# A linear-attention and gated-FFN block rewritten around a static list schedule: K and V first with in-place features, Q feature-major, attention output token-major

## The chip, the cores and the metric

Both kernels run on one core of one Trainium2 chip. The metric is the device time of one execution in microseconds (us). All outputs are right.

Five engines work side by side and meet through semaphores: TensorE (PE in the profile; PEld is its weight loads), VectorE (DVE), ScalarE (ACT), GpSimd (POOL), and SyncE (SP), which only issues DMAs. SPq and ACTq are the instruction streams in which SP and ACT issue them. Each engine works through the list that the program gives it, and in these traces an instruction that waits holds up what is listed behind it on that engine.

## The reference

With B=1, S=2048, D=640, H=32 heads of width 20, F=1536, all in bf16:

```python
def A(x, wqkv, w_phi, wo):                       # linear attention
    q, k, v = split_heads(x @ wqkv)              # each [H, S, 20]
    pq, pk = q @ w_phi, k @ w_phi                # per head, 20x20
    phi_q = concat(softmax(pq), softmax(-pq))    # softmax over the head's 20 features
    phi_k = concat(softmax(pk), softmax(-pk))
    kv  = phi_k^T @ v                            # [40, 20] per head, a sum over ALL tokens
    z   = phi_k.sum(tokens)
    o   = (phi_q @ kv) / (phi_q @ z + 1e-6)
    return merge_heads(o) @ wo

def B(x, w_gate, w_up, w_down):                  # bilinear gated FFN
    return ((x @ w_gate) * (x @ w_up)) @ w_down

h   = x + A(layernorm(x))
out = h + B(layernorm(h))
```

The sum over all tokens in `kv` is a barrier: no attention output exists before the last tile of K and V is done. Tokens are handled in 16 tiles of 128. Both kernels fold `w_phi` into the Q and K weights at the start ("the fold"), so that one projection gives `pq` and `pk` directly.

## The kernel before

The kernel is written by hand, engine by engine. Per tile, TensorE projects Q, K and V in one group of 1,920 columns. VectorE takes a row maximum of |pq| and |pk|, which ScalarE uses as the bias of four exponentials. VectorE then forms the feature sums of K and of Q, 1.39 to 1.41 us each, and their reciprocals. GpSimd normalises. The Q features are token-major at this point, so SyncE transposes them by two DMAs a tile.

```python
# SyncE: one semaphore "trq" counts both transposes of a tile
def trq(t):
    be = t % 3
    W(sy, "ex", 4 * t + 1)
    W(sy, "trq", 32 * t)                 # until BOTH transposes of tile t-1 have landed
    I(sy.dma_start_transpose(phiqT[:, 0, :, P*t:P*(t+1)], e_tmp[:, be, 0, :]), "trq", 16)
    W(sy, "nq", t + 1)
    W(sy, "trq", 32 * t + 16)            # until the first transpose of tile t has landed
    I(sy.dma_start_transpose(phiqT[:, 1, :, P*t:P*(t+1)], e_tmp[:, be, 1, :]), "trq", 16)

# VectorE
def emit_ss(t):
    ...
    dve.tensor_reduce(out=Ssum[:, b, 0:2*H], in_=phik[:, t, ...], op=ALU.add)          # K sums
    k = I(dve.tensor_reduce(out=Ssum[:, b, 2*H:4*H], in_=e_tmp[:, t%3, ...], op=ALU.add), "ss")  # Q sums
    ...                                                                               # reciprocals
for t in range(NT):
    W(dve, "prj", t + 1)
    I(dve.tensor_reduce(out=mx[:, t, :], in_=pp[:, 0:2*D]..., op=ALU.max,
                        apply_absolute_value=True, negate=True), "mx")
    if t >= 1:
        emit_ss(t - 1)

# ScalarE
W(act, "prj", t + 1)
W(act, "mx", t + 1)
W(act, "trq", 32 * (t - 2))              # e_tmp has three buffers
I(act.activation(out=e_tmp[:, be, 0, :], in_=pp[:, 0:D], func=ACT.Exp, bias=mx[:, t, 0:1], scale=1.0), "ex")
...                                      # three more exponentials, and the copy of V
```

After the barrier, the denominators (40 matmuls of 512 columns), their reciprocals, an expansion of the reciprocals to all features (20 matmuls), and the numerators (104 matmuls of 512 columns) are computed feature-major:

```python
# TensorE
ins = pe.matmul(bank(dbk)[H*b:H*(b+1), :], lhsT=Zsb[:, s, c, :], rhs=phiqT[:, s, c, cols], ...)        # 40 x
ins = pe.matmul(bank(1)[:, :], lhsT=GT4[:, b, P*i:P*(i+1)], rhs=rden2[:, b // 2, :], ...)              # 20 x
ins = pe.matmul(bank(nbk)[:, :], lhsT=KVsb[:, s, c, P*i:P*(i+1)], rhs=phiqT[:, s, c, cols], ...)       # 104 x
```

The output projection, the second layernorm and the FFN follow.

Of the kernel before, what the change touches and what calls it, by code (L numbers as in the profile page):

```python
# [7 lines left out]
I32 = mybir.dt.int32  # L8
ACT = mybir.ActivationFunctionType
# [10 lines left out]
E21 = DH + 1  # L20
F = 1536
NF = F // P
NB = S // 512
EPS_LN = 1e-5
EPS_DEN = 1e-6
MAGIC = 0x5F3759DF
NEWTON_ITERS = 3


def _chunk_heads(c):  # L30
    return (P * c) // DH, (P * c + P - 1) // DH


CH = [_chunk_heads(c) for c in range(NC)]


def _kchunks(i):
    lo, hi = CH[i]
    return [c for c in range(NC) if not (CH[c][1] < lo or CH[c][0] > hi)]


KC = [_kchunks(i) for i in range(NC)]
KV_GROUPS = [(c, s) for c in range(NC) for s in range(2)]


class SemPool:
    def __init__(self, nc, ctx):
        self.nc = nc
        self.ctx = ctx
        self.h = {}  # L50
        self.cnt = {}

    def add(self, name):
        self.h[name] = self.ctx.enter_context(self.nc.semaphore("s_" + name))
        self.cnt[name] = 0

    def inc(self, ins, name, by=1):
        ins.then_inc(self.h[name], by)
        self.cnt[name] += by
        return self.cnt[name]  # L60

    def wait(self, eng, name, val):
        if val <= 0:
            return
        eng.wait_ge(self.h[name], val)


def bass_sequential_preLN__linear_kernel_hedgehog__glu_gated_bilinear__prompt_kernel(
        nc, A_x, A_wqkv, A_w_phi, A_wo, B_x, B_w_gate, B_w_up, B_w_down, out, dbg=None):
    with ExitStack() as ctx:  # L70
        _build(ctx, nc, A_x, A_wqkv, A_w_phi, A_wo, B_w_gate, B_w_up, B_w_down, out, dbg or {})


build = bass_sequential_preLN__linear_kernel_hedgehog__glu_gated_bilinear__prompt_kernel


def _build(ctx, nc, A_x, A_wqkv, A_w_phi, A_wo, B_w_gate, B_w_up, B_w_down, out, dbg):
    def sb(shape, dt, name):
        return ctx.enter_context(nc.sbuf_tensor(name, shape, dt))

    x_all = sb([P, NT, D], BF16, "x_all")
    xnT = sb([P, NC, S], BF16, "xnT")
    Wp = sb([P, NC, 3 * D], BF16, "Wp")
    Wo_sb = sb([P, NC, D], BF16, "Wo_sb")
    BUFA = sb([P, 2 * NT * D], BF16, "BUFA")
    BUFB = sb([P, 2 * NC * S], BF16, "BUFB")
    vaug = sb([P, NT, H * E21], BF16, "vaug")
    KVsb = sb([P, 2, NC, D], BF16, "KVsb")
    Zsb = sb([P, 2, NC, H], BF16, "Zsb")
    G = sb([P, NC, H], BF16, "G")  # L90
    GT = sb([P, D], BF16, "GT")
    NXB = 3
    xn_tmp = sb([P, NXB, D], BF16, "xn_tmp")
    NEB = 3
    e_tmp = sb([P, NEB, 2, D], BF16, "e_tmp")
    st = sb([P, NT, 12], FP32, "st")
    mv = sb([P, NT, 2], FP32, "mv")
    vpe = sb([P, NT], FP32, "vpe")
    ysh = sb([P, NT], FP32, "ysh")
    rs = sb([P, NT], FP32, "rs")  # L100
    y2 = sb([P, NT], FP32, "y2")
    nb = sb([P, NT], FP32, "nb")
    st2 = sb([P, NT, 12], FP32, "st2")
    mv2 = sb([P, NT, 2], FP32, "mv2")
    vpe2 = sb([P, NT], FP32, "vpe2")
    ysh2 = sb([P, NT], FP32, "ysh2")
    rs2 = sb([P, NT], FP32, "rs2")
    y22 = sb([P, NT], FP32, "y22")
    nb2 = sb([P, NT], FP32, "nb2")
    mx = sb([P, NT, 2], FP32, "mx")  # L110
    Ssum = sb([P, 2, 4 * H], FP32, "Ssum")
    Rr = sb([P, 2, 3 * H], FP32, "Rr")
    rq = sb([P, 2, H], FP32, "rq")
    rden2 = sb([P, 2, 512], BF16, "rden2")
    RepQ = sb([P, NB, P], BF16, "RepQ")
    ident = sb([P, P], BF16, "ident")
    out_tmp = sb([P, 2, D], BF16, "out_tmp")
    tmp2 = sb([P, 2, 512], BF16, "tmp2")
    Wrows = sb([P, NC, DH], BF16, "Wrows")

    phik = BUFA[:, :].rearrange("p (t s n) -> p t s n", t=NT, s=2)
    Wqk_nat = BUFA[:, 0:NC * 2 * D].rearrange("p (c n) -> p c n", c=NC)
    Wgu = BUFA[:, 0:2 * NC * F].rearrange("p (g c n) -> p g c n", g=2, c=NC)
    GT4 = BUFA[:, 2 * NC * F:2 * NC * F + NB * D].rearrange("p (b n) -> p b n", b=NB)
    phiqT = BUFB[:, :].rearrange("p (s c n) -> p s c n", s=2, c=NC)
    WqkT = BUFB[:, 0:2 * NC * D].rearrange("p (w a n) -> p w a n", w=2, a=NC)
    Phi = BUFB[:, 2 * NC * D:3 * NC * D].rearrange("p (a n) -> p a n", a=NC)
    Wd_sb = BUFB[:, 0:NF * D].rearrange("p (f n) -> p f n", f=NF)
    HH0 = NF * D
    hhT = BUFB[:, HH0:HH0 + 2 * NF * 512].rearrange("p (b f n) -> p b f n", b=2, f=NF)  # L130
    vaug4 = vaug[:, :, :].rearrange("p t (h e) -> p t h e", e=E21)
    oT = vaug[:, :, :].rearrange("p t n -> p (t n)")[:, 0:NC * S].rearrange("p (c n) -> p c n", c=NC)
    h_all = x_all
    hnT = xnT
    hn_tmp = xn_tmp

    PPA = ctx.enter_context(nc.psum_tensor("ppa", [P, 2048], FP32))
    PPB = ctx.enter_context(nc.psum_tensor("ppb", [P, 2048], FP32))
    PPX = [PPA, PPB]

    def bank(k):
        return PPX[k // 4][:, 512 * (k % 4):512 * (k % 4 + 1)]

    def pair(k):
        return PPX[k // 4][:, 512 * (k % 4):512 * (k % 4 + 2)]

    def bank_bf(k):
        return bank(k).bitcast(BF16)

    PIECES = [(0, 512), (512, 1024), (1024, 1536), (1536, 1920)]  # L150

    SM = SemPool(nc, ctx)
    for name in [
        "xa", "xb", "xc", "xd", "w0", "w0k", "wv", "wphi", "wo", "wffn", "wd", "trx", "trq", "trh", "out0", "out1", "dbg",
        "gt4mm", "gt4", "wqk", "trp", "trev", "identr",
        "pool0", "nk", "nq", "kvm", "lnp",
        "ln1", "mx", "ss", "kvev", "rden", "oT", "h", "ln2", "hh", "outev",
        "wpev", "xn", "v", "ex", "hn", "rdx", "gsb",
        "wpmm", "prj", "kv", "den", "exd", "num", "att", "gu", "ffn",
    ]:  # L160
        SM.add(name)
    W = SM.wait
    I = SM.inc
    XS = ["xa", "xb", "xc", "xd"]

    with nc.Block("main") as block:

        @block.sync
        def _(sy):
            def xdma4(g4):  # L170
                I(sy.dma_start(x_all[:, 4 * g4:4 * g4 + 4, :],
                               A_x[0, 4 * P * g4:4 * P * (g4 + 1), :].rearrange("(t p) n -> p t n", p=P)), XS[g4], 16)

            I(sy.dma_start(Wrows[:, :, :], A_w_phi.rearrange("h d f -> (h d) f").rearrange("(a p) f -> p a f", p=P)), "wphi", 16)
            I(sy.dma_start(Wqk_nat, A_wqkv[:, 0:2 * D].rearrange("(c p) n -> p c n", p=P)), "wqk", 16)
            xdma4(0)
            I(sy.dma_start(Wp[:, :, 2 * D:3 * D], A_wqkv[:, 2 * D:3 * D].rearrange("(c p) n -> p c n", p=P)), "wv", 16)
            for g4 in range(1, 4):
                xdma4(g4)
            I(sy.dma_start(Wo_sb[:, :, :], A_wo.rearrange("(c p) n -> p c n", p=P)), "wo", 16)  # L180

            def trx(t):
                W(sy, "xn", t + 1)
                W(sy, "trx", 16 * t)
                I(sy.dma_start_transpose(xnT[:, :, P * t:P * (t + 1)], xn_tmp[:, t % NXB, :]), "trx", 16)

            def trq(t):
                be = t % 3
                W(sy, "ex", 4 * t + 1)
                W(sy, "trq", 32 * t)  # L190
                I(sy.dma_start_transpose(phiqT[:, 0, :, P * t:P * (t + 1)], e_tmp[:, be, 0, :]), "trq", 16)
                W(sy, "nq", t + 1)
                W(sy, "trq", 32 * t + 16)
                I(sy.dma_start_transpose(phiqT[:, 1, :, P * t:P * (t + 1)], e_tmp[:, be, 1, :]), "trq", 16)

            trx(0)
            trx(1)
            trx(2)
            for t in range(NT + 1):
                if t + 3 < NT:  # L200
                    trx(t + 3)
                if t >= 1:
                    trq(t - 1)

            W(sy, "kv", len(KV_GROUPS))
            I(sy.dma_start(Wgu[:, 0, :, :], B_w_gate.rearrange("(c p) n -> p c n", p=P)), "wffn", 16)
            I(sy.dma_start(Wgu[:, 1, :, :], B_w_up.rearrange("(c p) n -> p c n", p=P)), "wffn", 16)
            def trh(t):
                W(sy, "hn", t + 1)
                W(sy, "trh", 16 * t)  # L210
                I(sy.dma_start_transpose(hnT[:, :, P * t:P * (t + 1)], hn_tmp[:, t % NXB, :]), "trh", 16)

            for t in range(0, 8):
                trh(t)
# [33 lines left out]
        def _(dve):  # L248
# [111 lines left out]
            for t in range(0, 4): Hadd(t)  # L360
# [404 lines left out]
```

## Time and profile before

| | |
|---|---|
| device time, median of 3 runs | 352.82 us (350.19 to 356.75, the last a slow run) |
| span of the profiled execution | 352.5 us |
| TensorE busy | 310.5 us, so 42.0 us idle |
| loop over the 16 Q, K, V tiles | 29.5 to about 124 us |
| first FFN matmul | 188 us |

These are lines of the profile's page for the kernel before: busy time by engine, busy tenths of TensorE and VectorE in 40 slices of 8.8 us each, and the shares that each engine has in the chain of waits (the chain of work that ended last, followed back from the end).

```profile
PE 310.5 (88%) x1756; PEld 156.8 (44%) x1786; DVE 202.4 (57%) x330; ACT 140.7 (40%) x231; POOL 99.4 (28%) x185
PE   0797887887778778899997999999999999999996
DVE  0796799999997933758883735453133322333221
PE 61%; DVE 19%; POOL 8%; DMA 5%; ACT 3%; issue 3%; POOLq 0%; ACTq 0%; SPq 0%; DVEq 0%
```

From the sixth to the twelfth slice VectorE stands at 9 and TensorE at 7 or 8. VectorE looks like the pace of the tile loop. The chain of waits of the kernel before, inside that loop, says the same. Its columns are start, duration, and what ran.

```profile
60.53 1.48 DVE mx L286
62.02 1.39 DVE Ssum L273
63.41 1.41 DVE Ssum L275
...
64.84 0.55 DVE Rr L278
65.39 0.22 DVE Rr L279
...
65.75 1.48 DVE mx L286
```

From one `mx` to the next is 5.22 us, and VectorE is occupied through all of it.

The busy times by window tell how much room TensorE has in the loop. The columns are the window, its length, then busy time and count for PE, PEld, DVE, ACT and POOL, then the granted TensorE clock, the DMA share, and GB/s. Kernel before:

```profile
40.00:60.00 20.00, 16.58 (x78) 7.53 (x80) 19.46 (x22) 17.28 (x29) 10.74 (x6) 1.00 0.39 78
60.00:80.00 20.00, 16.24 (x77) 7.43 (x79) 19.76 (x24) 16.61 (x28) 14.34 (x8) 1.00 0.44 87
```

TensorE works 16 of 20 us here. The last two columns show that bandwidth is not the limit: the DMA engines are busy 39 to 44% of the time and move 78 to 87 GB/s, where the busiest slice of the same page has 364.

### The profile page before, as it was taken

How to read it: one execution, taken by the hardware profiler on the slowest of the kernel's cores; microseconds unless marked ns; L12 is line 12 of the kernel's file. 1: busy time of each engine (PE TensorE's matmuls, PEld its weight loads, DVE VectorE, ACT ScalarE, POOL GpSimd, SP SyncE). 2: the span in 40 equal slices, each digit the busy share in tenths (PEclk: the TensorE clock that was granted, in tenths of full speed). 3: DMA queues.
4: the chain of work that ended last, by engine and by line, in shares of the span. 5: the costliest groups of instructions: out<-in, count | busy, mean ns of one | idle time of the engine just before them, and what ended most of it. 6: DMA issues, size and time to landing. Idle time of an engine off the chain costs nothing.

```text
span 352.5 us, 4737 instructions
## 1 busy us (share of the span) xinstructions
PE 310.5 (88%) x1756; PEld 156.8 (44%) x1786; DVE 202.4 (57%) x330; ACT 140.7 (40%) x231; POOL 99.4 (28%) x185
## 2 busy tenths in 40 slices
PE   0797887887778778899997999999999999999996
PEld 0643333333333763344543445444544455444553
DVE  0796799999997933758883735453133322333221
ACT  1765878888857402332342525223212210222000
POOL 8977076776674740000320030030000000000000
PEclk9998999999998989999999999999999999999999
DMA  7923135354643339300020281100330001000111
GB/s 240 364 86 61 26 68 109 60 111 85 84 84 66 59 73 327 122 3 0 0 58 19 56 243 38 38 2 0 58 93 0 3 19 58 0 0 2 40 55 56
DMA packets 52935, 25.24 MB, mean 72 GB/s; under 512 B 44080, under 2 KB 50992, under 8 KB 52912
## 3 DMA queue, kind: packets, MB, share of 16 engines
q1 hardware_dynamic: 52912, 24.94, 27.8%
q8 instruction: 14, 0.23, 0.3%
q14 instruction: 9, 0.07, 0.1%
HBM read 11.82 MB, written 2.62 MB: 41 GB/s over the span
## 4 chain that ended last, share of the span: by engine, by line
PE 61%; DVE 19%; POOL 8%; DMA 5%; ACT 3%; issue 3%; POOLq 0%; ACTq 0%; SPq 0%; DVEq 0%
PE ppa L712 29%; PE ppb L728 11%; DVE mx L286 5%; DVE Ssum L273 5%; DVE Ssum L275 5%; PE ppa L677 5%; PE ppa L602 4%; PE ppb L693 4%; DMA xnT<-xn_tmp 3%; PE ppb L729 3%; DVE Rr L278 2%; DMA BUFB<-e_tmp 2%; POOL BUFB L398 2%; POOL KVsb L402 2%; PE ppa L610 1%
## 5 line engine op out<-in xcount | busy, mean ns | idle before, releaser
L712 PE MATMUL ppa<-xnT,BUFA 128*128 128x512 bf16 x470 | 103.7, 379 | 2.2 <-DMA xnT<-xn_tmp 1.7
L712 PEld LDWEIGHTS ppa<-xnT,BUFA 128*128 128x128 bf16 x480 | 46.7, 98 | 58.1 <-issue 2.0
L348 DVE TENSOR_TENSOR BUFB<-ppa,tmp 128x512 bf16<-128x512 f32 x48 | 33.2, 691 | 64.7 <-ACT tmp L532 63.7
L532 ACT ACTIVATE tmp<-ppa 128x512 bf16<-128x512 f32 x48 | 28.7, 597 | 102.7 <-PE ppa L712 102.7
L728 PE MATMUL ppb<-BUFB 128*128 128x512 bf16 x185 | 51.3, 379 | 0.0
L602 PE MATMUL ppa<-Wp,xnT 128*128 128x512 bf16 (+1 forms) x156 | 36.5, 392 | 11.2 <-ACT vaug L504 8.9
L729 PE MATMUL ppb<-BUFB 128*128 128x128 bf16 x192 | 42.1, 219 | 0.4
L602 PE MATMUL ppb<-Wp,xnT 128*128 128x512 bf16 (+1 forms) x157 | 33.2, 365 | 5.5 <-ACT vaug L504 4.0
L444 POOL TENSOR_TENSOR BUFA<-BUFA,Rr 128x1280 bf16<-128x1280 bf16 x16 | 37.7, 2355 | 0.0
L355 DVE TENSOR_TENSOR out_tmp<-ppb,x_all 128x640 bf16<-128x640 f32 x16 | 13.1, 823 | 38.3 <-PE ppb L729 32.4
L602 PEld LDWEIGHTS ppa<-Wp,xnT 128*128 128x128 bf16 x160 | 15.9, 103 | 31.5 <-issue 14.4
L438 POOL TENSOR_TENSOR e_tmp<-e_tmp,rq 128x640 bf16<-128x640 bf16 x16 | 20.3, 1269 | 33.8 <-DVE rq L281 33.8
L728 PEld LDWEIGHTS ppb<-BUFB 128*128 128x128 bf16 x192 | 18.8, 98 | 22.7
L414 POOL TENSOR_SCALAR rs<-ysh 128x4 int32<-128x4 int32 x8 | 1.5, 192 | 94.8 <-DVE ysh L258 94.4
L677 PE MATMUL ppa<-BUFB,KVsb 128*128 128x512 bf16 x103 | 25.7, 379 | 2.3 <-DVE rden L313 1.1
L602 PEld LDWEIGHTS ppb<-Wp,xnT 128*128 128x128 bf16 x160 | 15.1, 97 | 23.4 <-issue 7.9
L273 DVE TENSOR_REDUCE Ssum<-BUFA 128x64 f32<-128x1280 bf16 x16 | 23.6, 1476 | 0.0
L275 DVE TENSOR_REDUCE Ssum<-e_tmp 128x64 f32<-128x1280 bf16 x16 | 23.6, 1475 | 0.0
L693 PE MATMUL ppb<-Wo_sb,vaug 128*128 128x512 bf16 x77 | 21.6, 380 | 0.1
L250 DVE BATCH_NORM_STATS2 st<-x_all 128x6 f32<-128x320 bf16 x32 | 15.0, 468 | 10.5 <-DMA x_all<-in_A_x_dram 10.5
L729 PEld LDWEIGHTS ppb<-BUFB 128*128 128x128 bf16 x192 | 18.8, 98 | 0.4
L512 ACT ACTIVATE tmp<-ppa 128x512 bf16<-128x512 f32 x15 | 9.0, 597 | 24.2 <-PE ppa L671 14.5
(97 smaller groups left out, 387.6 us busy)
## 6 DMA issues: line engine op xcount, KB each, us to landing
x_all<-in_A_x_dram SPq DMA_DIRECT2D x4, 640.0 KB, 10.8
out_dram<-out_tmp SPq DMA_DIRECT2D x16, 160.0 KB, 1.8
BUFA<-in_B_w_gate_dram SPq DMA_DIRECT2D x1, 1920.0 KB, 8.7
BUFA<-in_B_w_up_dram SPq DMA_DIRECT2D x1, 1920.0 KB, 13.1
BUFB<-in_B_w_down_dram SPq DMA_DIRECT2D x1, 1920.0 KB, 9.1
BUFA<-in_A_wqkv_dram SPq DMA_DIRECT2D x1, 1600.0 KB, 7.3
Wp<-in_A_wqkv_dram SPq DMA_DIRECT2D x1, 800.0 KB, 10.3
Wo_sb<-in_A_wo_dram SPq DMA_DIRECT2D x1, 800.0 KB, 11.0
```

The costliest lines, as they stand in the source:

```text
L273: dve.tensor_reduce(out=Ssum[:, b, 0:2 * H], in_=phik[:, t, :, :].rearrange("p s (h f) -> p (s h) f", f=DH), axis=AX.X, op=ALU.add)
L275: k = I(dve.tensor_reduce(out=Ssum[:, b, 2 * H:4 * H], in_=e_tmp[:, t % 3, :, :].rearrange("p s (h f) -> p (s h) f", f=DH), axis=AX.X, op= ...
L348: ins = dve.tensor_tensor(out=hhT[:, hb, ft, :], in0=bank(gp + 1)[:, :], in1=tmp2[:, q % 2, :], op=ALU.mult)
L438: ins = pool.tensor_tensor(out=e_tmp[:, be, 1, :].rearrange("p (h f) -> p h f", f=DH), in0=e_tmp[:, be, 1, :].rearrange("p (h f) -> p h f" ...
L444: ins = pool.tensor_tensor(out=phik[:, t, :, :].rearrange("p s (h f) -> p (s h) f", f=DH), in0=phik[:, t, :, :].rearrange("p s (h f) -> p ...
L532: ins = act.activation(out=tmp2[:, q % 2, :], in_=bank(gp)[:, :], func=ACT.Copy)
L602: ins = pe.matmul(pp[:, n0:n1], lhsT=lhsT, rhs=Wp[:, c, n0:n1], start=(c == 0), stop=(c == NC - 1))
L677: ins = pe.matmul(bank(nbk)[:, :], lhsT=KVsb[:, s, c, P * i:P * (i + 1)], rhs=phiqT[:, s, c, cols], start=(n == 0), stop=(n == len(lst) - 1))
L693: pe.matmul(pair(ap_)[:, 0:512], lhsT=lhsT, rhs=Wo_sb[:, c, 0:512], start=(c == 0), stop=(c == NC - 1))
L712: ins = pe.matmul(bank(gp + gu)[:, :], lhsT=Wgu[:, gu, c, P * ft:P * (ft + 1)], rhs=hnT[:, c, cols], start=(c == 0), stop=(c == NC - 1))
L728: pe.matmul(pair(fp)[:, 0:512], lhsT=lhsT, rhs=Wd_sb[:, ft, 0:512], start=(ft == 0), stop=(ft == NF - 1))
L729: ins = pe.matmul(pair(fp)[:, 512:D], lhsT=lhsT, rhs=Wd_sb[:, ft, 512:D], start=(ft == 0), stop=(ft == NF - 1))
```

## The change

The intent is to remove TensorE work after the barrier, to take the maximum, the Q sums and the Q transposes out of the tile loop, and to leave the instruction order to a scheduler. The whole file is new. A graph of operations, each with an engine, an assumed duration, a priority (`key`; the lower goes first) and its data, is run through a list-scheduling simulation when the kernel is built. What comes out is a fixed order for each engine. The diff, cut to its core:

```diff
-    W(act, "mx", t + 1)                                  # row maximum as bias of the exponentials
-    I(dve.tensor_reduce(out=mx..., op=ALU.max, ...), "mx")
-    k = I(dve.tensor_reduce(out=Ssum[:, b, 2*H:4*H], in_=e_tmp...), "ss")      # Q feature sums
-    I(sy.dma_start_transpose(phiqT[:, 0, ...], e_tmp[:, be, 0, :]), "trq", 16) # Q features, 2 a tile
-    I(sy.dma_start_transpose(phiqT[:, 1, ...], e_tmp[:, be, 1, :]), "trq", 16)
-    DEN(...); RR(...); NUM(...)                          # denominators, reciprocals, numerators
+# K and V, tile by tile: exponential without a maximum, normalised in place by GpSimd
+    G.op("act", "Kx%d_%d" % (t, s), ... func=AF.Exp, scale=1.0 - 2.0*s ...)
+    G.op("dve", "Ks%d" % t, ... tensor_reduce(out=SR[.., 0, :], in_=ek) ..., 1.40, ...)
+    G.op("dve", "Kr%d" % t, ... reciprocal ..., 0.55, ...)
+    G.op("pool", "Kn%d" % t, ... ek *= 1/sum ...)
+    kvlast = G.op("pe", "KV%d" % t, ...)                 # 12 small matmuls, V carries a column of ones
+# Q, feature-major: the weights are the stationary operand; no sums, no transposes
+    ins = e.matmul(pb(b)[:, 0:n], lhsT=T["Wp"][:, 0, i, P*c:P*(c+1)], rhs=T["xnT"][:, i, o0:o0+n], ...)
+    G.op("act", "Qx%d_%d_%d" % (q, c, s), ... out=T["eqT"][:, s, c, o0:o0+n], func=AF.Exp ...)
+# attention, token-major: per head 20 values + the denominator + the feature sum = 22 columns
+    for (c, j0, j1, y) in NUMP:
+        ins = e.matmul(pb(b, y)[...], lhsT=T["eqT"][:, s, c, P*t:P*(t+1)], rhs=T["KVm"][...], ...)
+    sr, rho, A, B, dd, rd  ->  VectorE;   o -> GpSimd;   oT -> DMA transpose;   O -> output projection
+# the second layernorm's scale is applied at the very end (gate*up is quadratic in it)
+    y = (h2 @ w_down) * 1/(var + eps) + h
+# Q weights: transposed from DRAM by six DMAs, which depend on nothing
+    for g in range(6):
+        G.op("sp", "wqt%d" % g, lambda e, g=g: e.dma_start_transpose(out=T["wqT"][:, g:g+1, :],
+             in_=T["A_wqkv"][:, WIN[g]:WIN[g]+P]), 1.22, 2.6, [], [wqt_b[g]], key=55 + g, dma=-1)
+    dma("sp", "wg", ..., 1966, [wg_b], key=75)           # gate and up weights, 3.9 MB in all,
+    dma("sp", "wu", ..., 1966, [wu_b], key=76)           # which depend on nothing either
+    for i in range(NC):
+        fold(1, i, -88 + i, "act" if i % 2 else "dve")   # K weights
+    for i in range(NC):
+        fold(0, i, 62 + i, "act")                        # Q weights: needs all six wqt
```

In `1.22, 2.6` the scheduler is told that a DMA transpose occupies SyncE for 1.22 us and lands after 2.6 us.

## The prediction

> **What bounds it now.** The chain of waits gives TensorE 61% of the 352.5 us span and VectorE 19%. By stage (windows and timeline):
> - 0 to 29.5 us: weight folding for Q and K, cold and gapped; the first projection starts at 29.5.
> - 29.5 to 124 us: one VectorE tile cycle of 5.2 us (max 1.48, feature sums 1.39 + 1.41, reciprocals 0.55 + 0.22) paces 16 tiles; TensorE needs about 4 us of each.
> - 124 to 188 us: K/V sums, denominators with a 3.36 us reciprocal, numerators, output projection; the first FFN matmul waits on transposes of 2.6 to 4.1 us.
> - 188 to 349 us: FFN, TensorE solid, 0.219 us per 512-column matmul.
>
> **TensorE work, costed from the trace.** Back to back, 512 columns take 0.219 us, 512+128 take 0.273 (so 320 about 0.137), K/V sums about 0.067.
> - Removed: denominator, numerator and reciprocal-expansion matmuls, 164 x 0.219 = 36 us; 16,400 of the fold's 22,800 columns, about 7 us.
> - Added: 192 token-major numerator matmuls (1,584 columns a tile), about 11.5 us.
> - Kept: projections, output projection, FFN.
>
> After: K, V, output and FFN-down 864 x 0.1375 = 119; FFN-up 105; Q 22; K/V sums 13; numerators 11.5; set-up 7 to 8. Estimate 278 us, against 310 busy before.
>
> **VectorE.** The max goes; Q's sums become matmul columns. Per tile in the K/V stage: 1.40 + 0.55 + about 0.42, plus 1.15 for layernorm statistics, 2.4 to 3.5 us, below TensorE's 3.55 (K, V, sums). So that stage becomes TensorE-bound, with Q as filler. Attention costs VectorE about 5.5 us a tile (two 672-element PSUM operations near 0.86 each, residual 0.82, statistics 1.15, small operations, semaphore bubbles). It overlaps the FFN, where VectorE was a quarter busy. GpSimd's Newton steps leave the start.
>
> **What is lost.** The instruction order puts the gate and up weights (3.9 MB) on the SP queue before the transposes of tiles 2 to 15, and the Q-weight transposes before those. The Trainium skill, "DMA: Bandwidth & Descriptors", section "Queues, rings and completion order", says each DMA engine consumes a queue's descriptors in ring order. About 9.9 MB is issued ahead; before's busiest slice moved 364 GB/s. Tile 2 becomes ready only near 34 to 37 us (estimate), though TensorE has run dry near 26: about 10 us lost, partly at half rate (cold transposes were paced at 0.105 us, warm 128 columns at 0.055).
>
> **Sum.** 36 us, plus about 262 of remaining TensorE work, 5 in the step to attention (two 2.6 us transposes and some ten VectorE operations precede the first FFN matmul), 1 to 2 for the late down-weight load (9.1 us before), 3 at the end: 307 us. If queueing is harmless, about 297; if Q-weight transposes are slow or VectorE delays attention, up to 320. Nearly all of the 32 us TensorE saving is on the critical path; the rest is removed idle time.
>
> Prediction: 307 us, range 294 to 322. Faster by over 2%: 0.97; within 2%: 0.02; slower: 0.01.
>
> **Right or wrong if the profile shows:** TensorE pacing of 0.137/0.219 us, total near 278 us; from 40 us on above 95% TensorE; a TensorE gap of 5 to 12 us between tiles 1 and 2, released by a transpose; numerators near 0.7 us a tile; FFN matmuls starting near 120 us; chain of waits mostly TensorE.
>
> **What would make it wrong:** small matmuls (42 to 154 columns) paced well above 0.067 us by weight loads; strided PSUM reads slower than 0.86 us; a static in-order schedule stalling when real durations drift; a lower granted clock.

## More of the kernel before

Of the kernel before, one run in each of three batches was slow (356.75, 356.94 and 357.26 us); ratios are formed from fast runs alone, and the profiles are of fast runs.

The timeline of the DMA issues on SyncE, kernel before, shows the transposes of the Q features (L191 is the first of a tile, L194 the second):

```profile
64.01 1.20 SPq L194 DMA_TRANSPOSE BUFB<-e_tmp  x1
65.30 1.23 SPq L185 DMA_TRANSPOSE xnT<-xn_tmp  x1
66.65 1.20 SPq L191 DMA_TRANSPOSE BUFB<-e_tmp  x1
69.29 1.20 SPq L194 DMA_TRANSPOSE BUFB<-e_tmp  x1
```

L194 recurs after 5.28 us. L191 to L194 is 2.64 us, and so is L194 to L191.

## The result, and the profile after

| | before | after |
|---|---|---|
| device time, median of 4 runs each (one of before's was slow) | 352.86 us | 312.97 us (312.19 to 313.84) |
| ratio | | 0.890 (95%: 0.885 to 0.894) |
| profiled span | 352.5 us | 310.5 us |
| TensorE busy / idle | 310.5 / 42.0 us | 277.5 / 33.0 us |
| VectorE / ScalarE / GpSimd busy | 202.4 / 140.7 / 99.4 us | 177.6 / 107.5 / 66.6 us |
| first FFN matmul | 188 us | 116.2 us |

Ratios here and below are the mean time of one kernel's fast runs over that of the other's in the same rounds, so they are not quite the ratio of the quoted medians. Busy times of TensorE hold a few tenths of uncertainty, because a few matmul records are missing from some traces (1,756 recorded before; 1,786 in an experiment that leaves the matmuls alone).

The kernel is 11% faster. Of the 42.0 us of span, 33.0 are TensorE work that no longer exists and 9.0 are idle time. The same lines of the page, kernel after (a slice is now 7.8 us):

```profile
PE 277.5 (89%) x2041; PEld 182.9 (59%) x2058; DVE 177.6 (57%) x357; ACT 107.5 (35%) x189; POOL 66.6 (21%) x71
PE   3418699999999869979999999799999999999996
DVE  3743999956547697393645367758454743332332
PE 77%; DVE 8%; SPq 6%; DMA 4%; ACT 1%; issue 1%; POOL 1%; DVEq 0%
```

The chain is now three quarters TensorE. From the sixth slice on TensorE is nearly solid, but for a dent at the fourteenth to fifteenth slice and a small one at the eighteenth. The first five slices read 3, 4, 1, 8, 6: the start is where the new kernel loses most. The timeline of TensorE, kernel after, shows it (in brackets: idle time before the group, and what ended it):

```profile
12.15 0.47 PE L251 MATMUL ps<-Phi,scratch 120*128 120x120 bf16 x7 [1.16 <-ACT scratch L236]
22.49 1.22 PE L251 MATMUL ps<-Phi,scratch 120*128 120x120 bf16 x14 [9.88 <-DMA scratch<-in_A_wqkv_dram]
23.55 4.72 PE L326 MATMUL ps<-Wp,xnT 128*128 128x320 bf16 x20
...
37.07 5.89 PE L326 MATMUL ps<-Wp,xnT 128*128 128x320 bf16 x40 [1.79 <-DMA xnT<-xn]
```

Between 12.6 and 22.5 us TensorE stands still. L251 is the fold, and what it waits for is `scratch<-in_A_wqkv_dram`, the DMA transposes of the Q weights. The chain of waits, kernel after, shows why they come so late (SPq L181 is their issue):

```profile
4.36 4.27 SPq L181
...
8.68 4.41 SPq L181
...
13.13 2.31 SPq L181
...
15.48 2.42 SPq L181
...
17.94 1.27 SPq L181
...
19.26 3.10 DMA scratch<-in_A_wqkv_dram
...
22.49 1.22 PE ps L251 x14
...
33.54 3.48 DMA xnT<-xn
```

Six issues took SyncE 16.2 us (4.36 to 20.5), up to 4.4 us for one. The plan had assumed 1.22. The DMA of a Q-weight transpose took 5.6 us from issue to landing (the page's median of six) against the 2.6 assumed. The median hides the order: the six took 14.2, 10.3, 6.4, 4.9, 3.5 and 3.1 us, and they landed between 18.57 and 22.36 us. The DMA issues of the kernel after between 4 and 5 us (with KB each and us to landing) show the first, and a bulk load issued before it:

```profile
Wo<-in_A_wo_dram ACTq DMA_DIRECT2D x1, 800.0 KB, 15.6
scratch<-in_A_wqkv_dram SPq DMA_TRANSPOSE x1, 14.2
```

These output-projection weights, from ScalarE's queue, landed at 18.56 us, and no Q-weight transpose landed before. In all, some 5.1 MB (x, the K and V weights, these) had been issued ahead of the transposes. So the Q-weight transposes themselves seem to have stood behind bulk loads, in a place where the prediction did not look; no run takes those loads away alone.

The plan expected the Q weights by about 12.9 us, so it put two steps of Q's fold into TensorE's list ahead of the first K and V projections, although nothing needs Q so early. The other engines' lists are tied to this. The waits of ScalarE, kernel after, from 5 to 32 us (in all, times, longest) show that it stood behind the fold as well:

```profile
ACT Wp L261 <- PE ps L251: 13.5, 3, 11.1
```

Behind the fold's copy-out in ScalarE's list are the layernorm operations of tiles 4 to 7, then of 1, 2 and 3. VectorE needs them to normalise. So the first rows that go to a DMA transpose are finished only at 33.5 us. The planned order shows that they are those of tile 4: x of tiles 4 to 7 is loaded from ScalarE's queue, ahead of that of tiles 2 and 3, and the plan takes tile 4 third. The transpose itself takes only 3.48 us and lets TensorE go on at 37.07.

The group that starts near 23.6 us holds 4.57 us of the chain (23.72 to 28.29). The same twenty matmuls take 2.72 us from start to start later in this trace. The granted clock was 0.50 between 15 and 25 us, and 0.63 as a mean between 20 and 30. The Trainium skill, "TensorE: Matmul & The Clock Gate", section "Part 1: The HAM clock gate (the "warmup" mystery)", says that the array falls to half rate after an idle window of about 3.4 us and comes back after a busy one. This trace agrees with the half rate: a gap of 9.88 us, with a clock of 0.50 in it and after it. How long a wait it takes, these runs do not show (see wd_act below).

The busy times by window, kernel after, in the columns explained before:

```profile
40.00:60.00 20.00, 19.87 (x184) 15.18 (x186) 19.04 (x32) 12.54 (x23) 14.05 (x6) 1.00 0.41 68
60.00:80.00 20.00, 19.50 (x183) 14.87 (x181) 12.50 (x13) 11.62 (x18) 14.09 (x6) 1.00 0.09 17
...
100.00:120.00 20.00, 15.71 (x126) 10.29 (x126) 16.85 (x45) 8.75 (x16) 7.21 (x9) 1.00 0.41 59
120.00:140.00 20.00, 18.11 (x156) 14.12 (x154) 13.43 (x36) 7.72 (x16) 1.72 (x5) 1.00 0.36 43
```

The K/V loop now keeps TensorE at 97% or more where before had 82%. The step to attention, 100 to 120 us, is the one other place with a visible loss, 4.3 us. There TensorE waits in short pieces for VectorE, which computes the first attention tiles and layernorms while Q is nearly used up as filler.

### The profile page after: what moved, and what is told of

It reads as the page before. It is cut to its first block, busy times and chain, and to the rows that moved or that the text cites. A ratio compares the mean times of both kernels' runs of the same rounds, so it can differ in the third digit from the quotient of the medians.

```text
span 310.5 us, 4962 instructions
## 1 busy us (share of the span) xinstructions
PE 277.5 (89%) x2041; PEld 182.9 (59%) x2058; DVE 177.6 (57%) x357; ACT 107.5 (35%) x189; POOL 66.6 (21%) x71
## 4 chain that ended last, share of the span: by engine, by line
PE 77%; DVE 8%; SPq 6%; DMA 4%; ACT 1%; issue 1%; POOL 1%; DVEq 0%
PE ps L496 33%; PE ps L514 17%; PE ps L326 12%; PE ps L457 6%; PE ps L385 5%; SPq L181 5%; PE ps L366 3%; DVE xn L301 2%; PE ps L414 2%; DVE x_all L461 2%; DMA scratch<-scratch 1%; DMA xnT<-xn 1%; SPq L158 1%; DMA scratch<-in_A_wqkv_dram 1%; DVE st L468 1%
## 5 line engine op out<-in xcount | busy, mean ns | idle before, releaser
L496 PE MATMUL ps<-xnT,Wgu 128*128 128x512 bf16 (+1 forms) x589 | 104.8, 336 | 2.8 <-DVE rs L473 1.9
L496 PEld LDWEIGHTS ps<-xnT,Wgu 128*128 128x128 bf16 x600 | 58.4, 98 | 46.7 <-DVE ev L504 3.4
L504 DVE TENSOR_TENSOR ev<-ps,scratch 128x512 bf16<-128x512 f32 (+1 forms) x60 | 35.0, 584 | 49.4 <-PE ps L496 48.4
L501 ACT ACTIVATE scratch<-ps 128x512 bf16<-128x512 f32 (+1 forms) x60 | 30.7, 511 | 90.7 <-PE ps L496 90.7
L514 PE MATMUL ps<-Wp,ev 128*128 128x320 bf16 x384 | 53.5, 299 | 0.5 <-DVE ev L504 0.5
L326 PE MATMUL ps<-Wp,xnT 128*128 128x320 bf16 x320 | 48.3, 307 | 2.8 <-DMA xnT<-xn 1.8
L357 POOL TENSOR_TENSOR ev<-ev,SR 128x1280 bf16<-128x1280 bf16 x16 | 37.8, 2364 | 44.6 <-DVE SR L355 35.9
L514 PEld LDWEIGHTS ps<-Wp,ev 128*128 128x128 bf16 x384 | 37.3, 98 | 15.5 <-DVE ev L504 0.8
L326 PEld LDWEIGHTS ps<-Wp,xnT 128*128 128x128 bf16 x320 | 31.3, 100 | 15.6 <-DMA xnT<-xn 2.0
L349 ACT ACTIVATE ev<-ps 128x640 bf16<-128x640 f32 x32 | 20.8, 700 | 15.2 <-PE ps L326 15.2
L457 PE MATMUL ps<-Wo,scratch 128*128 128x320 bf16 x160 | 23.9, 299 | 1.5 <-DMA scratch<-scratch 0.9
L251 PE MATMUL ps<-Phi,scratch 120*128 120x120 bf16 (+3 forms) x70 | 5.0, 238 | 11.6 <-DMA scratch<-in_A_wqkv_dram 9.9
```

The lines of the kernel that those rows point to most:

```text
L326: ins = e.matmul(pb(b, hb)[:, 0:320], lhsT=T["xnT"][:, c, P * t:P * (t + 1)], rhs=T["Wp"][:, kind, c, 320 * hb:320 * (hb + 1)], start=(c = ...
L349: G.op("act", "Kx%d_%d" % (t, s), lambda e, s=s, b=b, ek=ek: e.activation(out=T["ek"][:, ek.slots[0], s, :].rearrange("p (b n) -> p b n", ...
L357: G.op("pool", "Kn%d" % t, lambda e, ek=ek, sr=sr: e.tensor_tensor(out=T["ek"][:, ek.slots[0], :, :].rearrange("p s (h f) -> p (s h) f", f ...
L457: ins = e.matmul(pb(b, hb)[:, 0:320], lhsT=T["oT"][:, oT.slots[0], c, :], rhs=T["Wo"][:, c, 320 * hb:320 * (hb + 1)], start=(c == 0), stop ...
L496: ins = e.matmul(pb(b)[:, 0:n], lhsT=T["Wgu"][:, gu, c, P * ft:P * (ft + 1)], rhs=T["xnT"][:, c, o0:o0 + n], start=(c == 0), stop=(c == NC ...
L501: G.op("act", "g%d_%d" % (bi, ft), lambda e, pg=pg, gt=gt, n=n: e.activation(out=T["gt"][:, gt.slots[0], 0:n], in_=pb(pg)[:, 0:n], func=AF ...
```

## The experiments

Every kernel was timed in rounds with the kernel before on the same chip; only ratios are compared across batches. The medians of the kernel before in the four batches were 353.66, 352.13, 353.74 and 353.65 us.

One caution holds for every edit of the new kernel. The scheduler re-plans the whole order when one priority or dependency changes. So each edit is one change of the source, and a set of small changes in the order.

### 1. What causes the loss at the start?

My theory was queue order: SyncE issues the gate and up weights before the first activation transpose, which then has to stand behind 3.9 MB. The trace after gave a rival: TensorE and ScalarE stand, in order, behind Q's fold. Three edits tell them apart. The first issues the gate and up weights after the last activation transpose. The second creates the Q-weight transposes and Q's fold after tile 6's transpose. The third does both.

```diff
 # w_late
-    dma("sp", "wg", ..., key=75);   dma("sp", "wu", ..., key=76)
+    dma("sp", "wg", ..., key=75, after=[G.by["xt15"]]);   dma("sp", "wu", ..., key=76, after=[G.by["xt15"]])
 # q_late: both moved below the code that creates xt0 to xt15
-    G.op("sp", "wqt%d" % g, ..., key=55 + g, dma=-1)
+    G.op("sp", "wqt%d" % g, ..., key=55 + g, dma=-1, after=[G.by["xt6"]])
 # qw_late: both edits
```

> The changed kernel, but the gate and up weights (3.9 MB) are issued only after the transpose of tile 15; nothing else moves. Theory W (the prediction's): the 10 us at the start are lost because tile 2's transpose queues behind these weights; then tile 2 is ready 8 to 10 us sooner than 37 us and the time falls by 8 to 10 us to about 304. Theory Q (from the trace after): TensorE and ScalarE stand in program order behind the fold of Q's weights, which waits 9.9 us for the last transposed Q weights; then this run changes nothing by more than 1.5 us, the gap before the fold stays near 10 us, and the transpose of tile 2 falls from 3.5 to about 2.7 us.

> The changed kernel, but the transposes of Q's weights are issued after the transpose of tile 6, and Q's fold, which needs them, falls behind the first K and V tiles in every engine's order. The gate and up weights are now even earlier on the queue. Theory Q: K and V of tile 0 start near 14 us instead of 23.6 and the time falls by 6 to 12 us. Theory W: tile 2 still comes only near 34 us, so the time falls by at most 3 us. If both hold in part, a TensorE gap of 3 to 8 us released by the transpose of tile 2 appears.

> Both moves together. Theory Q alone: as q_late within 1.5 us. Theory W alone: as w_late. If, with Q's fold out of the way, the weights on the queue are the next wait, this run is 3 to 6 us below q_late: about 299 us. The Q-weight transposes should land in about 3 us each on the emptier queue instead of 5.6.

| | median us | ratio to before (95%) |
|---|---|---|
| after, for comparison | 312.97 | 0.890 (0.885 to 0.894) |
| w_late | 313.53 | 0.889 (0.885 to 0.893) |
| q_late | 315.33 | 0.893 (0.889 to 0.897) |
| qw_late | 307.28 | 0.869 (0.863 to 0.876) |

With the weights late and nothing else, the gap stayed. The timeline of TensorE, w_late:

```profile
22.60 1.23 PE L249 MATMUL ps<-Phi,scratch 120*128 120x120 bf16 x14 [10.02 <-DMA scratch<-in_A_wqkv_dram]
```

The six Q-weight issues still took 16.0 us of SyncE. The first activation transpose still took 3.47 us, so the fall to 2.7 that I had expected did not come, and its delay is not due to the gate and up weights. With Q late and nothing else, the gap went from before the first projection to after it, and its cause changed. The chain of waits, q_late:

```profile
2.38 14.56 DMA x_all<-in_A_x_dram
...
18.23 11.01 DMA xnT<-xn
...
29.28 2.86 PE ps L327 x10
```

The first line is the load of x for tiles 8 to 15, issued by ScalarE. VectorE has tile 8's statistics in its list ahead of the normalisation of tile 4, so even the issue of tile 4's transpose came only at 18.23. Then the theory of queue order is right: the weights had been issued between 4.8 and 6.1 us, landing at 23.2 and 28.7, and the transpose landed after 11.0 us, where one that meets an empty queue takes 2.6. The Trainium skill, "DMA: Bandwidth & Descriptors", section "Queues, rings and completion order", says that on each DMA engine the descriptors of a queue are consumed in ring order; the landing just behind the weights agrees.

With both edits TensorE has work from 15.3 us on. The timeline of TensorE, qw_late:

```profile
15.32 8.31 PE L328 MATMUL ps<-Wp,xnT 128*128 128x320 bf16 x40 [1.61 <-DVE Wp L254]
...
31.40 5.89 PE L328 MATMUL ps<-Wp,xnT 128*128 128x320 bf16 x40 [0.95 <-DMA xnT<-xn]
```

What follows: in the kernel as changed, the start is lost to Q's fold, which stands early in every list and waits for its slow transposes. Queue order is a second obstacle of nearly the same size that lies hidden behind the first and comes out when the first is taken away. Removing one gains nothing; removing both gains about 2 points of the ratio, or 6 to 7 us (I had expected about 299 us for qw_late; it took 307.28). My prediction had the size of the loss and the wrong one of two causes.

The first K/V matmuls started 8 us earlier (15.3 against 23.6) and the third tile's 13 us earlier (23.8 against 37.1), yet the first attention matmul came at 88.2 us, against 94.9 after. So half of the head start was given back. In qw_late VectorE was busy 14.97 of the 15 us from 30 to 45 us: the early part of the K/V stage runs into VectorE, which has its layernorm statistics and feature sums to do.

### 2. Was VectorE the limit of the tile loop before?

The prediction said that one VectorE cycle of 5.2 us paced the loop. The rival is the serial pair of transposes. The first edit takes the maximum away (the changed kernel does without it too). The second lets the two transposes of a tile be in flight together, and waits only for the same half of the tile before. The third does both. None changes TensorE's work.

```diff
 # before_nomax
-    W(dve, "prj", t + 1)
-    I(dve.tensor_reduce(out=mx[:, t, :], ..., op=ALU.max, ...), "mx")
-    W(act, "mx", t + 1)
-    ... func=ACT.Exp, bias=mx[:, t, 0:1], scale=1.0)     # and the other three
+    ... func=ACT.Exp, scale=1.0)
 # before_2q
-    W(sy, "trq", 32 * t)          ... "trq", 16)
-    W(sy, "trq", 32 * t + 16)     ... "trq", 16)
+    W(sy, "trqa", 16 * t)         ... "trqa", 16)
+    W(sy, "trqb", 16 * t)         ... "trqb", 16)
 # before_nomax_2q: both edits
```

> The kernel before without the row maximum (the exponentials take no bias; the softmaxes are the same in exact arithmetic): one part of the change alone. If the VectorE tile cycle of 5.2 us paced the projection stage, as the prediction read it, the cycle falls by 1.48 us to 3.7, below TensorE's about 4.1, so the stage from 29.5 to 124 us shrinks by about 16 x 1.1 = 17 us and the time falls to about 336. If TensorE or the transposes paced it, the time stays within 4 us of 353.

> The kernel before, row maximum kept, but the two transposes of a tile's Q features count on a semaphore each, so that the second need not wait for the first to land. VectorE's tile cycle of 5.2 us is untouched. If VectorE paces before's projection stage (with the transposes' own 2 x 2.64 = 5.3 us a second limit of the same size behind it), the time stays within 2 us of before. If the serial transposes alone paced it, the time falls by 10 us or more.

> Both limits of the kernel before taken away: no row maximum (VectorE 3.7 us a tile) and the two transposes of Q's features overlapped. If there were two limits of equal size, VectorE and the serial transposes, the tile cycle falls to TensorE's 4.05 us or ScalarE's about 4.2, the stage shrinks by 14 to 17 us and the time falls to 336 to 340, though each removal alone gave 0 to 4. If a third thing paced it, the time stays above 345.

| | median us | ratio to before (95%) | TensorE busy / idle in the profile |
|---|---|---|---|
| before, for comparison | 352.86 | 1 | 310.5 / 42.0 us |
| before_nomax | 349.56 | 0.991 (0.986 to 0.995) | 306.4 / 40.9 us |
| before_2q | 349.21 | 0.991 (0.985 to 0.998) | 308.6 / 39.0 us |
| before_nomax_2q | 331.32 | 0.939 (0.933 to 0.945) | 305.9 / 23.6 us |

Without the maximum, VectorE idles and the loop keeps its pace, because the transposes hold it. The chain of waits, before_nomax, from 61 us on:

```profile
61.62 2.57 DMA BUFB<-e_tmp
...
64.26 2.57 DMA BUFB<-e_tmp
...
66.90 2.58 DMA BUFB<-e_tmp
```

Two of them make 5.28 us a tile. (Until about 57 us the loop did run faster, with TensorE at 19.55 of 20 us in the window from 40 to 60; the three buffers of Q features absorbed the lag for that long. The few us gained come from there. ScalarE first waited for a transpose at 54.83 us.) The busy times by window, before_nomax, show that no engine is then full:

```profile
60.00:80.00 20.00, 14.86 (x71) 6.64 (x71) 12.70 (x20) 14.53 (x26) 12.05 (x8) 1.00 0.49 90
```

With the transposes overlapped and the maximum kept, the cycle is VectorE's 5.21 us again (the time fell by 3 us, where I had expected at most 2). The chain of waits, before_2q:

```profile
64.07 1.49 DVE mx L286
...
69.29 1.48 DVE mx L286
```

Between 60 and 80 us VectorE was busy 19.72 of 20. With both edits the chain changes character. The chain of waits, before_nomax_2q, and then its busy times by window:

```profile
47.37 4.05 PE ppa L598 x20
51.42 4.05 PE ppb L598 x20
```

```profile
60.00:80.00 20.00, 20.00 (x100) 9.69 (x99) 18.94 (x26) 19.75 (x36) 17.67 (x11) 1.00 0.63 125
```

TensorE is full at 4.05 us a tile, with ScalarE (19.75 of 20) and VectorE (18.94) close behind. The time, 331.32 us, was better than the 336 to 340 that I had expected. What follows: the loop before had two limits of equal length, and each alone looked worthless to remove: 3 to 4 us each, 21 us together. The rewrite takes both away at once, since it has no maximum and never transposes Q features. A dozen edited lines get 21 us of the rewrite's 40. Of the 23.0 us by which the profiled span fell, 18.4 are idle time; the other 4.6 are busy time of the same matmuls (mean granted clock 0.981 before, 0.995 here; some records are missing as well).

This also corrects the reading of where the 42 us of span came from. From before_nomax_2q to the rewrite, TensorE's work falls by 28.4 us (305.9 to 277.5) but its idle time grows by 9.4 (23.6 to 33.0).

### 3. How much room has each engine in the new kernel?

The prediction said that VectorE is below TensorE's pace in the K/V stage, and that nearly all TensorE work lies on the critical path. The first edit issues every numerator matmul twice (the second pass starts the sums anew, so the result is right). The second adds one more feature sum of K per tile, into a buffer that nobody reads.

```diff
 # num_twice
-    for (c, j0, j1, y) in NUMP:
+    for (c, j0, j1, y) in NUMP * 2:
     ...
+        if (c, j0) == (0, 0):
+            seen = [True, True]
     ...
 # sums_twice
+    G.op("dve", "Kz%d" % t, ... tensor_reduce(out=T["SX"][:, t, :], in_=ek) ..., 1.40, LD, [ek], [sx], kk)
```

> The changed kernel with every numerator matmul issued twice (same result): 192 more matmuls, about 0.36 us per six, so 11.5 us more TensorE work. If TensorE bounds the kernel from 37 us on, as its chain of waits says, the time rises by 8 to 12 us (up to 4 us can hide in the TensorE gaps of the step to attention). If VectorE's attention work bounds it, the rise is below 4 us.

> The changed kernel with one more 1,280-element feature sum per K tile on VectorE (1.4 us each, 22 us in all, its result unused; output unchanged). If VectorE has the slack in the K/V stage that the prediction gave it (2.4 to 3.5 us a tile against TensorE's 3.55), about 17 us of the 22 hide and the time rises by 4 to 8 us. If VectorE were the limit there, it rises by about 20 us.

For num_twice: 318.78 us, ratio 0.904 (0.897 to 0.911). TensorE's busy time rose by 11.8 us (277.5 to 289.3), the profiled span by 6.6, and the time by about 5 (by the ratios; 5.8 by the medians of two batches): less than the 8 to 12 that I had expected. The rest went into idle time: from 100 to 140 us TensorE was busy 38.71 of 40 us, where after has 33.82, so 4.9 us of the added work fell into the step to attention, where TensorE had been waiting for VectorE. TensorE work in that stage is therefore not all on the critical path.

For sums_twice: 323.19 us, ratio 0.914 (0.909 to 0.919). The 16 added operations take 22.4 us of VectorE at 1.40 us each, which is also what the chain of before had from start to start. The time rose by about 8.4 by the ratios (10.2 by the medians, 11.0 in the profiled span), more than the 4 to 8 that I expected. So some 12 to 14 us of VectorE's time in the K/V stage was slack (less, if one counts by VectorE's total busy time, which rose by 17.6 as other operations got shorter). VectorE then needs 1.40 + 1.40 + 0.55, or 3.35 us a tile for the sums and reciprocals alone, which is TensorE's cadence of 3.40, before layernorm statistics. The planner filled TensorE's waits with Q's projections (89 of the 94 recorded Q matmuls came before the first attention matmul, in after 37 of 94), so that fewer were left to fill the step to attention, and the first attention matmul moved from 94.9 to 108.6 us. VectorE is the close second limit of the new K/V stage, closer than the prediction's "2.4 to 3.5 us" let it seem.

### 4. A faster order

Nothing in these edits changes what is computed; only the order changes, of loads and transposes and, through one priority, of numerators. best1 takes both edits of experiment 1 (Q after tile 3's transpose), loads x of tiles 1 to 3 ahead of the V weights, moves the output-projection weights behind tile 8's transpose (and to SyncE's queue), and gives the numerators of tiles 5 to 7 less priority, so that Q's projections are left to fill the step to attention.

```diff
 # best1
-    dma("sp", "wv", ..., key=-94)
+    dma("sp", "wv", ..., key=-91)
-    dma("act", "wo", ..., key=-58)
+    dma("sp", "wo", ..., key=58, after=[G.by["xt8"]])
-PRIO = {}
+PRIO = {"N%d_%d" % (t, s): 20 for t in range(5, 8) for s in range(2)}
     # and wqt after xt3, wg and wu after xt15
```

> The changed kernel with four moves of order, no other work: x tiles 1 to 3 ahead of V's weights, the output weights after the transpose of tile 8, Q's weights after the transpose of tile 3 and the gate and up weights after that of tile 15; and the numerators of tiles 5 to 7 lower in priority, so that Q's projections fill the step to attention. From qw_late (307.3): the start should gain 1 to 3 us more, the step to attention about 2 to 3 us: 301 to 304 us. Without effect of the last move the TensorE idle time in the step to attention stays near 4 us.

The result was 303.52 us, ratio 0.861 (0.856 to 0.867). TensorE was busy 19.29 us of the window from 100 to 120 (after: 15.71, though best1 reaches each stage some 8 us sooner, so the windows hold different work). But 120 to 140 fell to 15.81. The timeline of TensorE, best1:

```profile
138.18 1.53 PE L460 MATMUL ps<-Wo,scratch 128*128 128x320 bf16 x10 [2.80 <-DMA scratch<-scratch]
```

That wait is for the transpose of an attention tile. The chain of waits, best1, has the transpose:

```profile
130.96 7.17 DMA scratch<-scratch
```

It took 7.17 us instead of 2.6, because SyncE had issued the 1.9 MB of down weights at 129.34 just ahead of it. From 131 to 137 us the DMA engines moved 335 GB/s. The other attention transpose took 5.42 us. In the kernel after, the down weights were issued at 149.85 and no output-projection matmul waited more than 0.9 us for a transpose. I tried the other queue: the same load, issued by ScalarE.

```diff
 # wd_act: best1, and
-    dma("sp", "wd", ...)
+    dma("act", "wd", ...)
 # best2: wd_act, and
-    dma("sp", "wv", ..., key=-91)
+    dma("sp", "wv", ..., key=-92.5)     # V weights between x of tile 1 and x of tiles 2 and 3
-    xload("act", 8, 16, -59)
+    dma("act", "x8", ..., after=[G.by["L1s3"]])   # x of tiles 8 to 15 after tile 3's statistics
```

> best1 (303.5 us) with one change: the down weights are issued from ScalarE's queue instead of SP's. In best1 the transpose of an attention output, issued 1.6 us after the down weights on the same queue, took 7.2 us instead of 2.6 and TensorE stood 2.8 us for it. If a transpose has to pass behind the weights of its own queue, it now lands in 3 to 5 us (the two queues share the DMA engines), that TensorE wait falls below 1 us, and the time falls by 1.5 to 3 us, to about 301. If only the shared bandwidth mattered, nothing changes.

> wd_act and a different order of the first loads: x tile 1, V's weights, x tiles 2 and 3, and x tiles 8 to 15 only after the statistics of tile 3. In best1 TensorE waited 2.4 us for V's weights before the first V projection. Expected: that wait goes and the first projection starts near 14 us instead of 15.7, worth 1 to 2 us against wd_act: about 300 us. A late tile 8 to 15 could give it back in the K/V stage.

wd_act took 306.37 us, ratio 0.868 (0.865 to 0.871): not faster than best1, against my expectation, and probably slower (the intervals just overlap). The timeline of TensorE, wd_act:

```profile
134.00 2.29 PE L499 MATMUL ps<-xnT,Wgu 128*128 128x512 bf16 x5 [4.73 <-DMA xnT<-xn]
```

From ScalarE's queue the load was issued at 127.94, 1.4 us sooner, and now slowed the second transpose of the FFN's input, issued 0.3 us before it, which took 6.12 us; the first, which was not caught, took 2.58. In best1 both were ahead of the load in SyncE's order. The transposes of the attention output still took 6.44 and 4.71 us. Two things differ from best1, the queue and the time of issue, and no run separates them. The Trainium skill, "DMA: Bandwidth & Descriptors", section "Issuing engines are not separate DMA queues", says that DMAs run on the same 16 engines and interleave, whichever engine starts them. This agrees with it. The wait of 4.73 us also came with a lower clock: 0.83 from 120 to 140 us, where best1, whose longest wait there was 2.80 us, kept 1.00. But the length of one wait does not decide it: best1 itself stood at 0.50 from 16 to 20 us, after waits of 1.16 and 2.36 us with 0.47 us of matmuls between them, and sums_twice at 0.66 from 160 to 165, after waits of 1.53 and 1.46.

best2 took 307.87 us, ratio 0.874 (0.869 to 0.878). Its first projection did start at 11.88 us, 3.8 us sooner than in best1, where I had expected 1.7, but the first attention matmul came at 87.2 us (best1: 86.6), and the time is well above the 300 us that I had expected. The head start was lost to waits in the K/V stage that VectorE limits (it was busy 10.00 of 10 us from 30 to 40), and the down-weight load cost it a wait of 5.04 us, as in wd_act. The earlier start of TensorE was worth nothing here, because VectorE was behind.

best3 leaves the load on SyncE and cuts it into three pieces, each of which waits until the one before has landed.

```diff
 # best3: best1, and
-    dma("sp", "wd", lambda: T["Wd"], ..., 1966, [wd_b], key=310, after=lastproj)
+    for k in range(3):
+        dma("sp", "wd%d" % k, lambda k=k: T["Wd"][:, 4*k:4*k+4, :], ..., 655, [wd_p[k]], key=310,
+            after=lastproj + ([G.by["wd%d" % (k - 1)]] if k else []))
```

> best1 (303.5 us) with one change: the down weights come in three pieces of 0.64 MB, each issued when the one before has landed, with the two transposes of attention outputs between them. If a transpose behind a bulk load pays for the bytes ahead of it, these two now land in under 4.5 us each instead of up to 7.2, the TensorE wait of 2.8 us for them falls below 1 us, and the last piece lands near 141 us, so that the first FFN-down matmul may wait 1 to 2 us for it instead: between 1 and 3 us faster than best1, 300.5 to 302.5. If the pieces cost their own latency in series (about 2 us each), the gain is eaten and the time stays at 303 to 304.

The result was 302.03 us (301.02 to 303.12), ratio 0.856 (0.851 to 0.860). The timeline of TensorE, best3, at the places where best1 waited 2.80 us and where the down weights are first used:

```profile
138.66 1.53 PE L464 MATMUL ps<-Wo,scratch 128*128 128x320 bf16 x10 [0.26 <-DMA scratch<-scratch]
...
142.22 6.69 PE L521 MATMUL ps<-Wp,ev 128*128 128x320 bf16 x48 [0.95 <-DMA Wp<-in_B_w_down_dram]
```

The transposes took 3.59 and 4.74 us (I had expected under 4.5 each). The wait of 2.80 us became 0.26, at the cost of a wait of 0.95 for the last piece. TensorE was busy 18.36 us from 120 to 140. best3 beats both kernels: TensorE busy 279.0 and idle 20.8 us, against 277.5 and 33.0 after. Between best1 and best3 the intervals of the ratio overlap, so that last step is shown in the trace and only likely in the time.

## Why the prediction was right or wrong, point by point

**The time.** Predicted 307 us, range 294 to 322; measured 312.97.

**TensorE's work: right.** Predicted 278 us, measured 277.5. The pace that was read from before held: ten 320-column matmuls in 1.36 us (0.136 each), 512 columns in 0.219, the numerators 0.72 us a tile, the K/V sums 0.057 each (predicted 0.067).

**VectorE paced the loop before: incomplete.** The step that failed is "one VectorE tile cycle of 5.2 us paces 16 tiles". There were two cycles of 5.2 to 5.3 us, VectorE and the serial transposes. Experiment 2 showed it. It did no harm to the number only because the change removes both.

**"Nearly all of the 32 us TensorE saving is on the critical path; the rest is removed idle time": the sizes hold, the attribution does not.** Busy fell by 33.0 and idle by 9.0, as the sum said. But 21 us can be had without removing any TensorE work. The contributions depend on the order in which they are taken, and "TensorE's saving gave the gain" is one way of counting, not a cause.

**What is lost at the start: right size, by luck, and wrong cause.** The step that failed is "Tile 2 becomes ready only near 34 to 37 us" as a result of queue order. The first transposed tile did arrive at 37.07 (it was tile 4; I had not read the planned order closely enough), but its transpose took 3.48 us. TensorE stood 9.9 us in front of the fold of Q, ahead of tile 0, and not "between tiles 1 and 2"; at the third tile the wait was 1.79 us. The prediction named slow Q-weight transposes only as a tail risk ("up to 320"). They were the main term: 16.2 us to issue six. The predicted 10 us and the measured 9.9 are different waits. Queue order in the place predicted was real, but became visible only in q_late; loads ahead of the Q-weight transposes are in the trace, but were not tested alone.

**The K/V stage becomes TensorE-bound: right, with less margin.** TensorE was busy 19.5 to 19.9 of 20 us between 40 and 100 us. "From 40 us on above 95%" held: 96.3% between 40 and 300 us. But sums_twice shows VectorE within some 12 to 14 us of being the limit over the stage, and the faster orders ran into it.

**The step to attention: right.** Predicted 5 us, measured about 4 (4.3 us of idle from 100 to 120). The first FFN matmul was predicted near 120 and came at 116.2.

**The late down weights: wrong in kind, small.** Predicted 1 to 2 us. In the kernel after, no matmul of the down projection waited for them, and the 1.9 us of idle between 120 and 140 us were waits for VectorE's attention chain. The load became costly in best1 and wd_act, and not by landing late but by slowing transposes next to it.

**The remaining error of 6 us.** From 37.07 us on, 273.4 us of span were left; the prediction had 271.5 (262 + 5 + 1.5 + 3). The profiled span of 310.5 us exceeds 307 by the later arrival of the third tile (37 against the middle of 34 to 37) and these 2 us; the median of the timed runs is another 2.5 us above the profiled span. In the profiled execution of every kernel but before (where the record does not pair them) the device time exceeds the span by 1.7 to 2.1 us (in after, 312.41 for 310.5), and the prediction was a sum of spans; so about 1.9 of the 2.5 were left out by construction.

**What stays open.** Why six transposes from DRAM took 16.2 us to issue. They took 7.8 to 7.9 us in q_late and qw_late, where they came later and met less traffic (3.9 and 3.6 us to land, not 5.6). In after none landed before the last bulk load issued ahead of them. In q_late three activation transposes, issued behind the gate and up weights, also took 3.73, 3.53 and 2.80 us to issue. So slow issue goes with bulk loads ahead and is not peculiar to Q's weights, but no run isolates it. And since each edit of the schedule re-plans everything, the gain of best1 is not divided among its parts.

## What to carry to other kernels

When a loop's chain of waits names one engine, look for another cycle of the same length before costing its removal, and remove both before judging: here two edits gave 3 to 4 us each alone and 21 us together. A fixed instruction order is only as good as the durations it was planned with; put the measured cost of a DMA into the plan, above all for DMAs issued in the crowded start, and keep work that nothing needs yet (here Q's fold) behind work that everything needs. Here, moving a bulk load to another queue did not protect short transfers from it; issuing it in pieces that each wait for the last did in part (7.17 and 5.42 us became 3.59 and 4.74), and so did issuing it after the transfers that something waits for (2.6 us in qw_late, 11.0 in q_late).

## What the Trainium skill lacked or had wrong

- "DMA: Bandwidth & Descriptors", section "Latency and other measured facts", gives a bandwidth for DMA transposes (261 GB/s, or 350 to 400 if contiguous) but no latency. A transpose of one 128x640 bf16 tile, 164 KB, took 2.6 us from issue to landing on a quiet queue, which is 63 GB/s if each waits for the one before, as in the kernel before. Even overlapped, an issue of 1.22 us each allows at most 134 GB/s (164 KB in 1.22 us).
- The same page has no figure for a transpose near bulk loads. Here it took 4.7 to 8.2 us next to 1.9 MB of weights (best1, wd_act, after) and 11.0 us behind 3.9 MB (q_late). While it lasted the DMA engines were full (335 GB/s from 131 to 137 us in best1); the mean of a 20 us window, 132 GB/s, hides that.
- The same page, section "Issuing engines are not separate DMA queues", calls the sequencer time to start a DMA "usually small relative to the DMA itself". For transposes it was not: 1.2 us of 2.6 on a quiet queue, and an average of 2.7 us (up to 4.4) for the six Q-weight transposes on a loaded one, which blocked everything behind them on SyncE for 16.2 us.
- No page says that a transpose from DRAM is slower than one from SBUF: on the quieter queue of q_late and qw_late a 640x128 slice of the Q weights took 3.6 to 3.9 us (medians; the quickest 2.7 to 3.0, later ones of a series up to 5.3), against 2.6 to 2.7 for a 128x640 tile of activations of the same size.
- "TensorE: Matmul & The Clock Gate", section "Part 1: The HAM clock gate (the "warmup" mystery)", puts the fall of the clock after an idle window of about 3.4 us. Read as the length of one wait, that does not fit these runs: there was no fall in best1 after a wait of 2.80 us, but one to 0.50 after waits of 1.16 and 2.36 us with little work between, and one to 0.66 in sums_twice after 1.53 and 1.46. What else decides is not shown here.
